# Attention and two MLPs on one core: both first token blocks cut in two for the first MLP, two scalars spread by TensorE, and new order lists

## The chip, the core and the metric

The kernel runs on one core of a Trainium2 chip. The core has TensorE (PE) for matrix products, VectorE (DVE) and ScalarE (ACT) for elementwise work, GpSimd (POOL), SyncE (SP), whose queue issues all of this kernel's transfers, and 16 DMA engines that carry them out. The metric is device time in microseconds (us); the time shown is the median of several runs.

## The reference

Three stages follow each other, in float32.

```python
# 1: attention in chunks of 32 with a window; q, k, v: (4, 8, 768, 64), mem_k, mem_v: 8 rows a head
for c in range(24):
    k_full = concat(mem_k, k[c*32 - 16 : c*32 + 40])      # 8 + at most 56 rows
    v_full = concat(mem_v, v[c*32 - 16 : c*32 + 40])
    a = softmax(q_c @ k_full.T / 8)                        # with 1e-9 added to the sum
    out[c] = a @ v_full
x = out as (3072, 512)
# 2: first MLP; w_in (512, 2048), w_out (2048, 512), s and b are single numbers
r = maximum(x @ w_in, 0)
y = (s * r * r + b) @ w_out
# 3: second MLP; w_gate, w_val (512, 1536), w_out2 (1536, 512)
g = y @ w_gate
result = (g * sigmoid(g) * (y @ w_val)) @ w_out2
```

## The kernel before, in words

The attention works on 24 groups of 128 tokens. A group has six stages, each named by a letter in the lists: Q (queries transposed), T (keys transposed and spread into one window per chunk), S (scores, maximum, shift, exp, sums), A (probabilities transposed), V (product with the values, normalised), X (the result transposed and rounded into a high part `xhi` and a low part `xlo`). Three groups make a token block t of 384 tokens; there are eight blocks. Groups 0 to 5 load whole rows (`load_tokens`, one transfer list K) and transpose on PE; later groups load k and q in 12 parts (`load_quadrant`) and transpose on DVE (`turn_queries`, `turn_keys`). Values are loaded by `load_values` (V in the list of loads) into two buffers, group g into buffer g % 2.

The first MLP goes through 16 hidden blocks m of 128 for each token block t. An up product U (`first_up`, 12 matmuls: each float32 product is made of three with split operands, lines 560 to 562) gives `hp`. Then come relu (`first_relu`), the square with s and b (`first_square`), rounding to `ghi` (`round_hi`) and the rest `glo` (`residue`), and a down product D (`first_down`, 12 matmuls) adds to four accumulators `acc0` to `acc3`. Four accumulators exist, so one token block at a time can collect its sum. When a run of hidden blocks of one token block ends, `first_out` copies the accumulators to `y` and `first_store` writes them to DRAM, as a part (`part_dram`) if hidden blocks are left, else as `y_dram`; a part is loaded again (`load_part0`) and added at the end. Before the change block 0 is cut behind hidden block 5 (`PART = 6`), so that the order is (0, 0 to 5), (1, 0 to 15), (0, 6 to 15), and then blocks 2 to 7 whole.

A weight block m (W in the list of loads, `load_w1`: 512 KB of `w_in` and 512 KB of `w_out`) is used first when its hidden block first comes up. Before that `split` turns it into a high and a low part: magnitude (ACT or DVE, lines 840 and 842), bound (846), shift (850), sign (855), rest (862), rounding to the high part (229 or 231, ACT or DVE), and the low part (904), all but the named choices on DVE. All 16 stay in SBUF; each token block uses all of them. The second MLP comes after the eighth block and has weights and lists of its own.

The instructions are first collected as tasks with lengths (`plan.add`), dependencies and buffer rings, and a list scheduler (`Plan.run`) then fixes the order on every engine; on the chip each engine runs its own list in that order and waits on semaphores. PE's order is the order in which tasks are added: for the start it is written out in `START` (U and D stand for the next up and down product), and later `VISITS` says at which half step which stage of a group comes. `LOADS` gives the order of the first transfers on SP, each issued behind the one before it. `MOVED` names the tasks that go to the other engine than usual, with ACT or DVE as the choice (`either`): `r`, `s`, `g` with t_m are relu, square and rounding, `h_first` and `m_first` rounding and magnitude of a weight block, `k`, `m`, `q`, `a`, `x` the copies of a group, `y` the copies out of the accumulators. The numbers s and b are broadcast over 128 partitions by two small transfers (`load_consts`), which have no place in `LOADS`.

## Time and profile before

| | |
|---|---|
| median of 3 runs | 1234.26 us (1233.92 to 1235.15) |
| the profiled execution, its own time | 1235.41 us |
| its span, from the first to the last instruction | 1233.6 us |
| mean granted TensorE clock | 0.989 |
| PE, DVE, ACT busy | 1189.7, 773.4, 506.3 us |

Busy times are those of the one profiled execution, and so are all start times, counted from the start of its span. Matmuls are pipelined, so the PE column tells when PE has work, not how well its array is used. PE idles or waits where its busy time in a window is less than the window.

### The profile page before, as it was taken

What the parts mean: (1) busy time and instruction counts of PE and PEld (TensorE: products, weight loads), DVE (VectorE), ACT (ScalarE), POOL (GpSimd) and SP (SyncE); (2) the same over time, 40 slices, a digit from 0 to 9 for tenths busy, and PEclk for the clock granted to TensorE, in tenths of its full rate; (3) what the DMA queues carried; (4) which work ended last, traced back from release to release, by engine and by line L of the source; (5) the groups of instructions that cost most, each with busy time, mean ns of one, the idle gap of its engine ahead of it and who ended that gap; (6) DMA issues with size and microseconds to landing.
All of it is one profiled execution on the core that took longest, in us unless ns stands there. A gap on an engine that the chain in (4) does not pass through costs nothing.

```text
span 1233.6 us, 25831 instructions
## 1 busy us (share of the span) xinstructions
PE 1189.7 (96%) x10296; PEld 1129.8 (92%) x10296; DVE 773.4 (63%) x1496; ACT 506.3 (41%) x1018; POOL 22.8 (2%) x54
## 2 busy tenths in 40 slices
...
GB/s 191 219 120 190 104 123 43 62 52 67 44 51 63 42 67 45 51 91 1 156 219 96 187 198 188 188 227 282 263 187 187 183 182 299 207 186 188 188 114 93
DMA packets 217128, 174.11 MB, mean 141 GB/s; under 512 B 157487, under 2 KB 188719, under 8 KB 215471
## 3 DMA queue, kind: packets, MB, share of 16 engines
...
q14 instruction: 41, 0.33, 0.1%
HBM read 124.40 MB, written 47.97 MB: 140 GB/s over the span
## 4 chain that ended last, share of the span: by engine, by line
PE 79%; SPq 9%; DMA 6%; DVE 3%; issue 2%; ACT 1%; DVEq 0%; ACTq 0%
PE chain_a L560 6%; PE chain_a L561 6%; PE chain_a L562 6%; PE oacc L561 5%; PE oacc L560 5%; PE oacc L562 5%; PE acc L560 5%; PE acc L561 5%; PE acc L562 5%; PE hp L560 5%; PE hp L562 5%; PE hp L561 5%; PE chain_b L561 4%; PE chain_b L562 4%; PE chain_b L560 4%; SPq L350 3%
## 5 line engine op out<-in xcount | busy, mean ns | idle before, releaser
L560 PE MATMUL acc<-ghi,w_first 128*128 128x384 f32 x512 | 176.0, 344 | 3.0 <-DVE ghi L231 1.8
L560 PE MATMUL hp<-xhi,w_first 128*128 128x384 f32 x512 | 175.7, 343 | 0.7 <-ACT xhi L229 0.7
L561 PE MATMUL acc<-glo,w_first 128*128 128x384 f32 x512 | 173.2, 338 | 2.5 <-DVE glo L622 1.1
L561 PE MATMUL hp<-xlo,w_first 128*128 128x384 f32 x512 | 172.6, 337 | 1.1 <-DVE xlo L553 1.1
L562 PE MATMUL hp<-xhi,w_first 128*128 128x384 f32 x512 | 172.5, 337 | 0.0
L562 PE MATMUL acc<-ghi,w_first 128*128 128x384 f32 x512 | 172.3, 337 | 0.0
L748 ACT ACTIVATE kept<-chain_a 128x256 f32<-128x256 f32 x216 | 83.0, 385 | 163.4 <-PE chain_a L562 134.4
L600 DVE SCALAR_TENSOR_TENSOR r<-r,s_sb 128x384 f32<-128x384 f32 x92 | 57.0, 620 | 107.8 <-ACT r L589 105.1
L589 ACT ACTIVATE r<-hp 128x384 f32<-128x384 f32 x96 | 47.1, 491 | 186.1 <-PE hp L562 179.1
L560 PE MATMUL oacc<-w_down,ghi 128*128 128x512 f32 x288 | 114.1, 396 | 0.1
L561 PE MATMUL oacc<-w_down,ghi 128*128 128x512 f32 x288 | 114.1, 396 | 0.0
L562 PE MATMUL oacc<-w_down,glo 128*128 128x512 f32 x288 | 112.0, 389 | 0.0
L560 PEld LDWEIGHTS acc<-ghi,w_first 128*128 128x128 f32 x512 | 96.8, 189 | 5.9 <-DVE ghi L231 2.8
L561 PEld LDWEIGHTS acc<-glo,w_first 128*128 128x128 f32 x512 | 97.0, 189 | 5.4 <-DVE glo L620 3.1
L560 PEld LDWEIGHTS hp<-xhi,w_first 128*128 128x128 f32 x512 | 97.3, 190 | 2.2 <-ACT xhi L229 0.9
L561 PEld LDWEIGHTS hp<-xlo,w_first 128*128 128x128 f32 x512 | 97.4, 190 | 1.3 <-DVE xlo L553 1.3
L562 PEld LDWEIGHTS hp<-xhi,w_first 128*128 128x128 f32 x512 | 97.1, 190 | 0.0
L562 PEld LDWEIGHTS acc<-ghi,w_first 128*128 128x128 f32 x512 | 96.8, 189 | 0.0
L765 DVE TENSOR_TENSOR v<-v,g 128x256 f32<-128x256 f32 x144 | 61.0, 424 | 52.3 <-ACT g L761 50.4
L753 DVE TENSOR_TENSOR v<-chain_b,kept 128x256 f32<-128x256 f32 x144 | 61.0, 423 | 41.5 <-PE chain_b L562 26.8
L773 DVE TENSOR_TENSOR glo<-v,ghi 128x256 fp32r<-128x256 f32 x144 | 60.6, 421 | 36.6 <-ACT ghi L229 36.6
L560 PE MATMUL chain_a<-y,hi_up 128*128 128x256 f32 x288 | 81.3, 282 | 0.6 <-ACT kept L748 0.5
...
## 6 DMA issues: line engine op xcount, KB each, us to landing
...
```

The lines of the kernel that those rows point to most:

```text
L350: nc.sync.dma_start(out=qin[:, j], in_=q[b, h, s0:s0 + GQ, ds].rearrange("(n t) i -> t n i", t=QUAD))
L560: nc.tensor.matmul(o, whi, xhi, start=first, stop=False, skip_group_check=onto)
L561: nc.tensor.matmul(o, whi, xlo, start=False, stop=False, skip_group_check=onto)
L562: nc.tensor.matmul(o, wlo, xhi, start=False, stop=last, skip_group_check=onto)
L589: nc.scalar.activation(out=r, in_=hp, func=AF.Relu)
L600: nc.vector.scalar_tensor_tensor(out=r, in0=r, scalar=s_sb[:, 0:1], in1=r, op0=ALU.mult, op1=ALU.mult)
L748: nc.scalar.activation(out=t, in_=st2[n]["A"], func=AF.Copy)
L753: nc.vector.tensor_tensor(out=t, in0=st2[n]["B"], in1=st2[n].pop(f"a{i}"), op=ALU.add)
L765: nc.vector.tensor_tensor(out=v, in0=v, in1=g, op=ALU.mult)
L773: nc.vector.tensor_tensor(out=lo, in0=st2[n].pop(f"v{half + 1}"), in1=st2[n][f"hi{half}"].bitcast(F32), op=ALU.subtract)
```

## The change

Both token blocks 0 and 1 are now cut in two, and the order of the hidden blocks is (0, 0 to 3), (1, 0 to 7), (0, 4 to 15), (1, 8 to 15), then blocks 2 to 7 whole as before. Block 1 gets a part in DRAM of its own, stored behind hidden block 7 and loaded and added at the end.

s and b are loaded as one number each into a tile of one partition, by two transfers that stand first in `LOADS` (C). Two matmuls with one row (`spread_consts`) spread them over 128 partitions into PSUM, and DVE copies them to SBUF. PE runs these two first.

For a group that `MOVED` names with e (group 1), the shift by the maximum, the exp and the sums are done by eight ACT instructions, one for each head, with the negative maximum as bias and the sum as second output; DVE makes the negative maximum, and keeps only the last two small operations of the sums.

`START`, `VISITS`, `LOADS` and `MOVED` are new. Of MOVED, with names for the first two blocks and six groups, these go: a1, g0_5, g0_6, g0_10, g0_11, g0_15, g1_0, g1_2, g1_5, g1_9, g1_10, g1_11, h_first1, h_first6, h_first9, h_first12, h_first14, k2_0, k3_0, k4_0, m1_0, m2_0, m4_1, m_first0, q2, q4, r0_0, r0_12, r0_13, r1_5, s0_11, s0_12, s0_13, s1_2, s1_3, x4, y1_15_1, y1_15_2. These come: e1, g0_7, g0_14, g1_4, g1_12, g1_13, h_first10, k0_0, k1_1, k3_1, k5_0, k5_1, m2_1, m3_0, m5_0, m_first4, m_first7, m_first14, q3, r0_14, r1_3, r1_11, r1_14, s0_3, s0_4, s0_5, s0_6, s0_14, s1_0, s1_8, s1_9, s1_13, s1_15, x0, y0_3_0, y0_3_1, y0_3_3, y1_7_0. The usual engine of s0_4 and s0_5 changes from ACT to DVE.

```diff
@@ -28,35 +28,36 @@
 
 
 START = (
-    "Q0 T0 S0 Q1 A0 V0 T1 S1 X0 Q2 T2 A1 S2 V1 X1 A2 V2 Q3 T3 X2 S3 U U Q4 D T4 U A3 S4 D V3 "
-    "U D A4 Q5 T5 X3 U V4 X4 D U S5 D A5 D V5 X5 U "
+    "Q0 T0 S0 Q1 T1 A0 V0 S1 Q2 T2 S2 A1 X0 V1 A2 X1 V2 Q3 X2 U U D T3 D S3 Q4 U A3 V3 T4 U "
+    "X3 S4 D Q5 A4 V4 T5 S5 X4 D A5 V5 X5 U "
 )
 
 VISITS = {
-    (True, 0): (-3, -4, -3, 1, 8, 15),
-    (True, 1): (2, 6, 9, 15, 17, 18),
-    (True, 2): (10, 16, 17, 22, 25, 31),
+    (True, 0): (-10, -6, -3, 1, 6, 15),
+    (True, 1): (-1, 10, 9, 15, 21, 23),
+    (True, 2): (11, 9, 21, 26, 29, 31),
     (False, 0): (-8, -2, -3, 2, 8, 11),
     (False, 1): (6, 6, 8, 12, 18, 21),
     (False, 2): (10, 18, 18, 25, 29, 30),
 }
 
 LOADS = (
-    "W0 K0 W1 V0 K1 K2 W2 V1 W4 V2 K3 W3 V3 K4 W6 K5 W5 V4 W8 V5 W7 W10 W9 "
+    "C K0 V1 K1 W0 V0 K2 V2 W3 W1 K3 W2 V4 K4 W5 V3 K5 W4 V5 W6 W7 W8 W10 W9 "
 )
 
 MOVED = (
-    "a1 a11 a12 a2 a6 g0_10 g0_11 g0_13 g0_15 g0_2 g0_3 g0_4 g0_5 g0_6 g1_0 g1_10 g1_11 g1_15 "
-    "g1_2 g1_3 g1_5 g1_8 g1_9 g2_1 g2_10 g2_12 g2_15 g2_2 g2_3 g2_6 g2_7 g2_8 g3_0 g3_1 g7_1 "
...
+    "a11 a12 a2 a9 e1 g0_13 g0_14 g0_2 g0_3 g0_4 g0_7 g1_12 g1_13 g1_15 g1_3 g1_4 g1_8 g2_0 "
+    "g2_1 g2_10 g2_12 g2_15 g2_2 g2_3 g2_6 g2_7 g2_8 g3_0 g3_1 g7_1 g7_11 g7_15 g7_3 g7_7 "
...
 )
 
 
@@ -189,7 +190,8 @@
     GPB = T // GQ
     NG = NB * GPB
     NSUB = T // P
-    PART = 6
+    SEGMENTS = ((0, 0, 4), (1, 0, 8), (0, 4, M1), (1, 8, M1), *((t, 0, M1) for t in range(2, NB)))
+    SPLIT = {t: [a for n, a, z in SEGMENTS if n == t and a] for t in range(NB)}
     CH = 2 * 512
     TS = 512
     TH = TS // 2
@@ -212,10 +214,11 @@
 
     ident = const.tile([P, P], F32, name="ident")
     make_identity(nc, ident)
-    s_sb = const.tile([P, 1], F32, name="s_sb")
-    b_sb = const.tile([P, 1], F32, name="b_sb")
+    sb_in = const.tile([1, 2], F32, name="sb_in")
+    sb = const.tile([P, 2], F32, name="sb")
+    s_sb, b_sb = sb[:, 0:1], sb[:, 1:2]
     y_dram = [dram.tile([P, KD, T], F32, name=f"y_dram{t}") for t in range(NB)]
-    part_dram = dram.tile([P, KD, T], F32, name="part_dram")
+    part_dram = {t: dram.tile([P, KD, T], F32, name=f"part_dram{t}") for t in range(NB) if SPLIT[t]}
     sum_dram = [
         [dram.tile([P, TS // P, DM], F32, name=f"sum_dram{h}_{s}") for s in range(NS)] for h in range(PASSES - 1)
     ]
@@ -253,8 +256,17 @@
         raw1[m] = load_slot((w_in[:, cols], w_out[cols, :]), f"first{m}")
 
     def load_consts():
-        for dst, src in ((s_sb, s_in), (b_sb, b_in)):
-            nc.sync.dma_start(out=dst, in_=src.unsqueeze(0).to_broadcast([P, 1]))
+        for n, src in enumerate((s_in, b_in)):
+            nc.sync.dma_start(out=sb_in[:, n:n + 1], in_=src.unsqueeze(0))
+
+    spread = []
+
+    def spread_consts():
+        spread.append(ps_h.tile([P, 512], F32, tag="h", name="spread")[:, 0:2])
+        for n in range(2):
+            nc.tensor.matmul(
+                spread[0][:, n:n + 1], sb_in[:, n:n + 1].to_broadcast([1, P]), ident[0:1, 0:1], start=True, stop=True
+            )
 
     def weight1(m, n):
         w = w1[m]
@@ -487,6 +499,19 @@
         sc = staged[g]["sc"].rearrange("p j e s -> p (j e s)")
         nc.scalar.activation(out=sc, in_=sc, func=AF.Exp, scale=SCALE)
 
+    def stage_below(g):
+        staged[g]["nb"] = nb = ap_.tile([P, 2, NP, 1], F32, tag="nb", name=f"nb{g}")
+        nc.vector.tensor_scalar(nb, staged[g].pop("mx"), -SCALE, None, op0=ALU.mult)
+
+    def stage_exp_heads(g, e):
+        if e == 0:
+            staged[g]["rc"] = ap_.tile([P, NP, 2, 1], F32, tag="rc", name=f"rc{g}", bufs=2)
+        for j in range(NP):
+            nc.scalar.activation(
+                out=scores_to(g)[:, j, e], in_=staged[g]["s"][e][:, j], func=AF.Exp, scale=SCALE,
+                bias=staged[g]["nb"][:, e, j], accum_out=staged[g]["rc"][:, j, e],
+            )
+
     def stage_probs(g, early):
         sc = staged[g]["sc"]
         ps = bank(ps_acc, "acc3", f"psA{g}") if early else bank(ps_a, "a", f"psA{g}")
@@ -516,12 +541,14 @@
         stage_values(g, both)
         stage_scores(g + 1, both)
 
-    def stage_sums(g):
-        staged[g]["rc"] = rc = ap_.tile([P, NP, 2, 1], F32, tag="rc", name=f"rc{g}", bufs=2)
-        flat = rc.rearrange("p j e o -> p (j e o)")
-        nc.vector.tensor_reduce(
-            out=flat, in_=staged[g]["sc"].rearrange("p j e s -> p (j e) s"), op=ALU.add, axis=AX.X
-        )
+    def stage_sums(g, done=False):
+        if not done:
+            staged[g]["rc"] = ap_.tile([P, NP, 2, 1], F32, tag="rc", name=f"rc{g}", bufs=2)
+        flat = staged[g]["rc"].rearrange("p j e o -> p (j e o)")
+        if not done:
+            nc.vector.tensor_reduce(
+                out=flat, in_=staged[g]["sc"].rearrange("p j e s -> p (j e) s"), op=ALU.add, axis=AX.X
+            )
         nc.vector.tensor_scalar(flat, flat, 1e-9, None, op0=ALU.add)
         nc.vector.reciprocal(flat, flat)
 
@@ -567,10 +594,10 @@
 
 
     def begins(t, m):
-        return m == 0 or (t == 0 and m == PART)
+        return m == 0 or m in SPLIT[t]
 
     def ends(t, m):
-        return m == M1 - 1 or (t == 0 and m == PART - 1)
+        return m == M1 - 1 or m + 1 in SPLIT[t]
 
     def first_up(t, m):
         whi, wlo = weight1(m, 0)
@@ -595,12 +622,12 @@
         r, _ = g_t[t, m]
         if engine == "ACT":
             nc.scalar.activation(out=r, in_=r, func=AF.Square)
-            nc.scalar.activation(out=r, in_=r, func=AF.Identity, scale=s_sb[:, 0:1], bias=b_sb[:, 0:1])
+            nc.scalar.activation(out=r, in_=r, func=AF.Identity, scale=s_sb, bias=b_sb)
         else:
             nc.vector.scalar_tensor_tensor(
-                out=r, in0=r, scalar=s_sb[:, 0:1], in1=r, op0=ALU.mult, op1=ALU.mult
-            )
-            g_t[t, m] = r, b_sb[:, 0:1]
+                out=r, in0=r, scalar=s_sb, in1=r, op0=ALU.mult, op1=ALU.mult
+            )
+            g_t[t, m] = r, b_sb
 
     def round_hi(engine, t, m):
         r, bias = g_t[t, m]
@@ -635,18 +662,18 @@
 
     def first_out(engine, t, m, i):
         y = gp.tile([P, T], F32, tag="r", name="y")
-        if t == 0 and m == M1 - 1:
+        if t in parts:
             nc.vector.tensor_tensor(out=y, in0=acc[t, i], in1=parts[t][:, i], op=ALU.add)
         else:
             copy(engine, y, acc[t, i])
         y_t[t, i] = y
 
     def first_store(t, m, i):
-        nc.sync.dma_start(out=(y_dram[t] if m == M1 - 1 else part_dram)[:, i, :], in_=y_t.pop((t, i)))
-
-    def load_part0():
-        parts[0] = wp.tile([P, KD, T], F32, tag="w", name="part")
-        nc.sync.dma_start(out=parts[0], in_=part_dram)
+        nc.sync.dma_start(out=(y_dram[t] if m == M1 - 1 else part_dram[t])[:, i, :], in_=y_t.pop((t, i)))
+
+    def load_part(t):
+        parts[t] = wp.tile([P, KD, T], F32, tag="w", name="part")
+        nc.sync.dma_start(out=parts[t], in_=part_dram[t])
 
     y_t = {}
     sp = None
@@ -981,6 +1008,13 @@
             t = plan.add(PE, 1.00, lambda: stage_scores(g), at_[g]["t"], take=["a", "a"], give=["kt", "qt"])
         t = plan.add(DVE, 0.34, lambda: stage_max(g, 0), [t])
         t = plan.add(DVE, 0.34, lambda: stage_max(g, 1), [t])
+        if f"e{g}" in moved:
+            t = plan.add(DVE, 0.07, lambda: stage_below(g), [t])
+            for e in range(2):
+                t = plan.add(ACT, 1.0, lambda e=e: stage_exp_heads(g, e), [t], give=give, take=own if e == 0 else ())
+            at_[g]["n"] = t
+            at_[g]["rc"] = plan.add(DVE, 0.22, lambda: stage_sums(g, True), [t])
+            return t
         for e in range(2):
             t = plan.add(DVE, 0.34, lambda e=e: stage_shift(g, e), [t], give=give, take=own if e == 0 else ())
         at_[g]["n"] = plan.add(ACT, 0.54, lambda: stage_exp(g), [t])
@@ -1036,8 +1070,8 @@
     split1 = {}
     g_ready = {}
     acc_free = []
-    part_stored = []
-    part_loaded = []
+    part_stored = {}
+    part_loaded = {}
     y_stored = {}
 
     def plan_w1(m):
@@ -1055,16 +1089,18 @@
         )
         e = either(f"r{t}_{m}", {ACT: 0.52, DVE: 0.47}, lambda e: first_relu(e, t, m), [u], take=["r"], give=["h"])
         e = either(
-            f"s{t}_{m}", {ACT: 1.30, DVE: 0.56} if t == NB - 1 or (t == 0 and m < PART) else
+            f"s{t}_{m}", {ACT: 1.30, DVE: 0.56} if t == NB - 1 or (t == 0 and m < SEGMENTS[0][2]) else
             {DVE: 0.56, ACT: 1.30}, lambda e: first_square(e, t, m), [e, consts],
         )
         e = either(f"g{t}_{m}", {ACT: 0.55, DVE: 0.47}, lambda e: round_hi(e, t, m), [e], take=["ghi"])
         g_ready[t, m] = plan.add(DVE, 0.52, lambda: residue(DVE, t, m), [e], take=["glo"], give=["r"])
 
     def plan_down1(t, m):
-        added = t == 0 and m == M1 - 1
+        added = m == M1 - 1 and SPLIT[t]
         if added:
-            part_loaded.append(transfer([*part_stored, split1[M1 - 1]], load_part0, 1, 768, ["w"]))
+            part_loaded[t] = transfer(
+                [*part_stored[t], split1[M1 - 1]], lambda: load_part(t), 1, 768, ["w"], name=f"part{t}"
+            )
         outs = []
         for i in range(KD):
             last = i == KD - 1
@@ -1081,14 +1117,14 @@
             e = either(
                 f"y{t}_{m}_{i}", {DVE: 0.5} if added else {DVE: 0.5, ACT: 0.43} if i % 2 else
                 {ACT: 0.43, DVE: 0.5}, lambda e, i=i: first_out(e, t, m, i),
-                [outs[i], *(part_loaded if added else ())], take=["r"],
+                [outs[i], *([part_loaded[t]] if added else ())], take=["r"],
             )
             acc_free.append(e)
             stored = transfer([e], lambda i=i: first_store(t, m, i), 1, 192, give=["r"])
             if m == M1 - 1:
                 y_stored[t, i] = stored
             else:
-                part_stored.append(stored)
+                part_stored.setdefault(t, []).append(stored)
         if added:
             plan.add(DVE, 0.01, None, acc_free, put=["w"])
 
@@ -1225,11 +1261,10 @@
             plan.add(DVE, 0.01, None, partial[h, s], put=["w"], give=["so"])
 
 
-    consts = transfer([], load_consts, 2, 1)
-    order = (
-        [(0, m) for m in range(PART)] + [(1, m) for m in range(M1)] + [(0, m) for m in range(PART, M1)]
-        + [(t, m) for t in range(2, NB) for m in range(M1)]
-    )
+    consts = transfer([], load_consts, 2, 1, name="C")
+    consts = plan.add(PE, 0.10, spread_consts, [consts], take=["h"])
+    consts = plan.add(DVE, 0.10, lambda: nc.vector.tensor_copy(sb, spread[0]), [consts], give=["h"])
+    order = [(t, m) for t, a, z in SEGMENTS for m in range(a, z)]
     ups = downs = 0
     for item in START.split():
         what, g = item[0], int(item[1:] or 0)
```

## Rows read from the trace of the kernel before

**Rows 1.** The page: busy time of the engines, share of the span, instructions.
```profile
PE 1189.7 (96%) x10296; PEld 1129.8 (92%) x10296; DVE 773.4 (63%) x1496; ACT 506.3 (41%) x1018; POOL 22.8 (2%) x54
```

**Rows 2.** Windows: us, busy PE, PEld, DVE, ACT, POOL (instructions), granted clock, DMA share, GB/s.
```profile
0.00:20.00 20.00, 5.00 (x83) 4.36 (x84) 12.47 (x23) 4.64 (x5) 2.85 (x12) 1.00 0.88 207
20.00:40.00 20.00, 12.03 (x288) 9.72 (x287) 14.41 (x32) 5.87 (x10) 2.16 (x6) 0.92 0.77 179
...
60.00:80.00 20.00, 17.71 (x286) 15.74 (x284) 19.62 (x35) 12.26 (x21) 0.00 (x0) 1.00 0.57 140
80.00:100.00 20.00, 15.32 (x193) 13.79 (x194) 18.88 (x34) 8.13 (x12) 0.00 (x0) 0.87 0.47 119
...
sum 160.00, PE 124.72 PEld 113.49 DVE 135.43 ACT 69.98 POOL 13.46; mean PE 15.59 PEld 14.19 DVE 16.93 ACT 8.75 POOL 1.68
...
97.00:168.00 71.00, 68.16 (x544) 64.09 (x545) 64.74 (x95) 32.90 (x49) 8.46 (x12) 0.98 0.53 147
sum 168.00, PE 132.56 PEld 120.41 DVE 143.36 ACT 72.01 POOL 13.46; mean PE 44.19 PEld 40.14 DVE 47.79 ACT 24.00 POOL 4.49
...
169.00:546.00 377.00, 374.58 (x3961) 367.06 (x3960) 196.63 (x400) 125.46 (x226) 9.29 (x24) 1.00 0.28 58
```

**Rows 3.** Waits of PE, 160 to 640 us: in total, times, longest.
```profile
PE acc L560 <- DVE ghi L231: 1.6, 1, 1.6
```

**Rows 4.** Timeline of PE: start, us, instruction, [idle before <- releaser].
```profile
8.34 1.09 PE L415 MATMUL psQ<-ident,qk 128*128 128x128 f32 x4 [8.34 <-DMA qk<-in_q_dram]
...
36.12 1.48 PE L511 MATMUL psV<-v,at 64*32 64x64 f32 x37 [2.43 <-DMA v<-in_v_dram]
...
50.59 0.69 PE L560 MATMUL hp<-xhi,w_first 128*128 128x384 f32 x1
...
97.15 0.44 PE L560 MATMUL hp<-xhi,w_first 128*128 128x384 f32 x1 [0.69 <-ACT xhi L229]
...
168.00 0.33 PE L560 MATMUL hp<-xhi,w_first 128*128 128x384 f32 x1
...
176.32 0.33 PE L560 MATMUL hp<-xhi,w_first 128*128 128x384 f32 x1
```

**Rows 5.** Timeline of SP's queue: start, us, issue.
```profile
3.02 0.44 SPq L285 DMA_DIRECT2D qk<-in_q_dram  x1
...
27.79 0.40 SPq L257 DMA_DIRECT2D s_sb<-in_moe_s_dram  x1
...
29.81 7.36 SPq L401 DMA_DIRECT2D v<-in_v_dram  x8
...
153.43 0.39 SPq L240 DMA_DIRECT2D raw_first<-in_moe_w_in_dram  x1
...
170.29 1.50 SPq L649 DMA_DIRECT2D part<-part_dram  x1
```

**Rows 6.** Groups by line and shape, 0 to 97 us: busy us, mean ns.
```profile
L855 DVE SCALAR_TENSOR_TENSOR raw_first<-raw_first,t_first 128x1024 uint32<-128x1024 uint32 x9 | 11.0, 1220 | 0.2
...
L850 DVE TENSOR_SCALAR t_first<-t_first 128x1024 uint32<-128x1024 uint32 x9 | 6.2, 690 | 0.2
...
L229 ACT ACTIVATE kt<-psK 128x64 f32<-128x64 f32 x6 | 1.4, 225 | 2.5 <-DVE kt L231 2.5
...
L598 ACT ACTIVATE r<-r,b_sb,s_sb 128x384 f32<-128x384 f32 x5 | 3.5, 709 | 0.2
```

**Rows 7.** Timeline of DVE.
```profile
159.95 0.69 DVE L846 TENSOR_SCALAR t_first<-t_first 128x1024 f32<-128x1024 f32 x1 [2.24 <-ACT t_first L840]
...
166.54 1.22 DVE L904 TENSOR_TENSOR w_first<-raw_first,w_first 128x1024 fp32r<-128x1024 f32 x1
```

**Rows 8.** Windows of 2.5 us, columns as in rows 2.
```profile
32.50:35.00 2.50, 1.19 (x65) 0.89 (x64) 2.40 (x7) 0.23 (x1) 0.00 (x0) 1.00 1.11 361
35.00:37.50 2.50, 1.32 (x37) 1.07 (x37) 2.46 (x7) 1.11 (x2) 0.00 (x0) 0.85 1.00 140
```

**Rows 9.** Window behind the waits of step 6.
```profile
97.00:102.00 5.00, 3.76 (x12) 3.51 (x13) 4.50 (x5) 1.27 (x3) 0.00 (x0) 0.66 0.95 282
```

19 rows, old and new, of the table MOVED are left out of this document.

## The prediction

> **What bounds the kernel now.** I read the page first: TensorE (PE) is busy for 96% of the span, so only its gaps can be won [rows 1]. The windows show where they are: up to 160 us PE works 124.7 us, so 35.3 us are idle, 15 of these in the first 20 us, 8 in the second, 2.3 in 60 to 80 and 4.7 in 80 to 100; from 169 to 546 us it idles 2.4 us of 377 [rows 2], with one wait of 1.6 us as the longest [rows 3]. So the argument is about the first 180 us. I call one up product with its down product a step; (t, m) is token block t with hidden block m, W0 to W15 are the weight blocks, and steps are numbered from 0 in the order in which they run.
>
> PE's own rows, in order of time, show what the start is made of [rows 4]. The first transpose waits until 8.34 us for group 0's q, the values of group 1 land for 36.12, and the first up product starts at 50.59. Step 6, which is (1,0) and needs all of block 1's x, starts at 97.15 behind a wait on ACT for that x. Step 21, the first use of W15, starts at 168.00, and step 23 at 176.32: 8.32 for two steps, so 2.08 us a product at full clock. Two engines stand behind these. SP needs 7.36 us to issue V2's eight loads, of 0.4 each when nothing is in the way [rows 5]. And VectorE (DVE) is busy 19.6 of 20 us in 60 to 80 [rows 2]: each weight block costs it five passes over 128x1024, two like L850 (0.69) and three like L855 (1.22) [rows 6]; the last pass of the last block begins at 166.54 and takes 1.22 [rows 7]. PE asks for that block at 168.00, so DVE is just in time there and sets the pace.
>
> **The change, part by part.**
>
> *Loads.* Ahead of V2 the old list has W0, W1, W2 and W4 (4.2 MB), the new one W0 alone. Ahead of V5 the old one has eight weight blocks, the new one six. The bytes taken out are the quick ones: with the 16 DMA engines full, weights landed at 361 GB/s in one window, where values landed at 140 in the next [rows 8]. So 3.1 MB less in front of V2 buy 3.1/0.34 = 9 us. By the mean of 207 and 179 GB/s of the first two windows [rows 2] it would be 16; but K3 (below), behind two weight blocks, would then land at 42, and the first up product would start at 45. The Trainium skill says why the two differ ("DMA: Bandwidth & Descriptors", Specifications and Why small descriptors are slow: pieces under 512 B miss line rate, and a head's row here has 256 B); the trace agrees, with 140 against 361.
>
> SP in the new order, at 0.44 an issue [rows 5]: C two issues, K six, W two, V ten or eight with stalls. C to 1.6, K0 to 4.3, V1 to 9, K1 to 11.5, W0 to 12.5, V0 to 18.5, K2 to 21. V2 reuses V0's buffer and waits for V0's product, about 22.3, so it goes to 26; W3 and W1 to 28, K3 to 30.6. Behind 2.1 MB of weights at 0.34 MB/us and its own 0.6 MB, K3 lands near 37.5.
>
> *The start.* PE's order ends "V2 Q3 X2 U". V0 lands near 20.5, and for the chain of products and copies from there to group 2's values I allow 16 us; the old run came to group 1's values at 36.12 because they landed only then [rows 4]. So Q3 runs at 37.5, X2 at 38.4, and behind it and the two x copies, 2.1 us together by estimate, the first up product starts at 40.5 instead of 50.59: 10.1 us earlier. T3 and S3, done before it in the old order, come behind it now: 1.6 us by estimate, two stages of some 0.8. Net 8.5. Bounds: 37 (K3 no obstacle, gain 12) and 46 (V loads stall as V2 did, gain 3).
>
> *x of block 1.* It is needed at step 4 instead of 6. From 50.59 to 97.15 PE had 12 products of 2.08 and 15 stages of attention to do, at some 0.8 each 12 us: 37 of 46.6 us: 9.6 us were lost to DVE. The new stretch has 8 products, the 12 and the 1.6: 30.3 us, so by PE alone step 4 could start at 70.8. DVE's prices: a weight block 4.7 (its five passes, 5.04, times 0.93, since neighbours overlap by some 0.08 each). Up to 97 us it did 143.4 - 64.7 = 78.6 us of work [rows 2]; 43 passes (four kinds nine times, one seven [rows 6]) and two roundings take 42, five steps 6, so a group of attention 30.6/6 = 5.1. From 97 to 168, 38 passes and five roundings take 39, 1.6 groups 8, and the other 18 over 15 steps are 1.2 a step. From 40.5 it then has to do a rest of W1 (2), W2 and W3 (9.4), three groups (15.5), four steps (4.8) and a copy: 32.2 us, 34 to 36 at the 91 to 96% at which it ran. Step 4 starts at 75.5. Less the two steps that come later (8.35), the old 97.15 corresponds to 88.8: gain 13.3 there.
>
> *W15.* It is wanted at step 23 instead of 21. DVE did 143.4 us of work up to 168 [rows 2]. The new order adds two steps (2.4). The new lists, counted by name for the first two blocks, take from DVE 4 roundings of weights and 2 q or at copies (0.68 each), 6 roundings of g (0.35), a net squaring with scale (0.62) and for group 1 two shifts and a sum (1.4), and give it 2 magnitudes (0.69) and 2 k copies (0.62): 5.6 times 0.93 less. That makes 140.6. DVE's idle time was 24.6: 13.1 in the first 40 us and 11.5 behind them [rows 2]. In the new order the first 40 us hold fewer weights to fill them with (15 idle), and behind I take 5 to 13. W15 is ready between 161 and 169; I take 166, nearer the old share. Gain 176.3 - 166 = 10. This is less than the 13.3 at step 4, so it counts: PE gives some 3 us back in steps 16 to 23, where each step wants 4.7 plus 1.2 us of DVE and takes PE some 4.4.
>
> *s and b.* Two issues move from 27.8 [rows 5] to the head: 0.8 us of SP ahead of K0, contained in the sum. The two one-row products and the copy of two columns stand in no row. Below, nothing: PE idles until group 0 lands at 8.34 [rows 4]. Above, a copy of 0.22 [rows 6] for each of the three, 0.7, if a late landing of C takes that cover away. I take nothing.
>
> *Group 1's exp by heads.* Eight ACT instructions of 128x64. The nearest row, a copy of that size, takes 0.22; one with two pointer operands takes 0.71 at 128x384 [rows 6]: 1.8 to 3 us ahead of A1, in place of two shifts and one exp, some 1.4. K3 lands only at 37.5, so I take nothing; without that cover it would be 0.4 to 1.6.
>
> *Second split.* Block 1 is cut too: four more stores, a load of 1.5 on SP [rows 5], four adds in place of copies, one more change of accumulators. At the old changes PE has another up product in between, which hides it. I take nothing. The load of block 0's part is now close: it waits for the slot that W15's split frees, and its sum is wanted some 8 us behind that. Bounds 0 and 3 us, the latter if group loads stand before it on SP.
>
> *Later blocks.* Same work, and the lists hardly differ. The group loads on SP start perhaps 4 us earlier while PE is 10 earlier. The stall of 1.6 [rows 3] may go, others may come: plus or minus 2.
>
> **Sum.** The profiled run took 1235.4 us for a span of 1233.6, 1.2 over the median of 1234.3. 1235.4 - 10 = 1225.4, against the median 1224.3. I say 1225.
>
> **The rivals.**
>
> *DVE loses it to late loads.* It waited 2.24 us for W15's load [rows 7] and 6.3 in all from 97 to 168 [rows 2]. If that comes to 9 or 10, and PE's waits are each followed by a slow stretch as from 97 to 102 (granted 0.66, so part of it at 1.2 of the 2.4 GHz [rows 9], some 1.7 us lost), W15 is ready at 169 to 171 and the gain is 3 to 6: 1229 to 1232. For it: ten blocks instead of eight now come behind V5, on a queue that also carries the group loads. Against: two steps more of slack. The Trainium skill names the slow stretches ("TensorE: Matmul & The Clock Gate", Part 1: idleness halves the clock, work restores it); the trace agrees, at 0.66 behind the waits of step 6.
>
> *Slower: W15 issued too late.* It was issued at 153.43 and ready at 167.76: 14.3 us [rows 5, 7]. If the new plan issues it after 162, behind ten weights, a part's load and the group loads on the same queue, it is ready after 176.3 and the whole gain is gone; each us more is a us lost. Issued at 165 to 172, it gives 1237 to 1244. Against: SP reaches the group loads earlier, with V5.
>
> *More: DVE is not the limit.* If it idles only 10 us before 40, W15 is ready by 160, and step 4's gain of 13, or 16 with a start at 38, counts: 1218 to 1221.
>
> **How the numbers follow.** Forecast, 1221 to 1229: 0.48. More: 0.14. Gain lost, 1229 to 1234: 0.20. Slower: 0.18. A measurement of this kernel tells about 0.2% from no change, 2.5 us, so faster means under 1231.8: 0.48, 0.14 and just over half of the third, 0.73. Within: 0.10. Slower: 0.17. Likeliest 1225, by itself 1221 to 1229. For 8 in 10 I leave out a little of "more" and the far half of "slower": 1217 to 1238.
>
> **What would show it.** Right: group 0's first transpose at 6.5 to 8; first up product near 40; step 4 near 75; DVE over 93% busy from 60 to 160; W15's last pass ending near 166 with step 23 right behind it; PE idle up to 160 us near 25 in place of 35. Wrong: a first up product past 46, with PE waiting on v or qk loads; DVE idle before a weight's first pass; PE waits on block 0's part or on r buffers at a change of accumulators; new waits past 200 us behind the turning of keys.

## Result and profile after

The changed kernel took 1241.12 us (median of 5 runs, 1239.87 to 1243.8) beside 1234.26 of the kernel before (5 runs, 1232.25 to 1235.56): ratio 1.006, 95% interval 1.0045 to 1.0075. It is 7 us slower, where 1225 was forecast and 1238 was the end of the range. The profiled execution took 1243.8 for a span of 1242.0, 8.4 us over that of before.

The windows of after, columns as in [rows 2]:

```profile
0.00:20.00 20.00, 8.34 (x102) 6.81 (x102) 7.65 (x19) 4.40 (x7) 5.55 (x18) 1.00 0.71 156
20.00:40.00 20.00, 12.37 (x345) 9.53 (x342) 13.72 (x30) 6.85 (x23) 0.40 (x1) 0.92 0.79 198
...
60.00:80.00 20.00, 15.04 (x266) 13.58 (x256) 17.94 (x34) 7.14 (x15) 0.00 (x0) 0.83 0.64 166
80.00:100.00 20.00, 15.03 (x184) 13.49 (x184) 18.77 (x33) 8.81 (x14) 0.00 (x0) 0.74 0.45 131
...
sum 160.00, PE 125.37 PEld 114.36 DVE 132.94 ACT 75.05 POOL 14.59; mean PE 15.67 PEld 14.30 DVE 16.62 ACT 9.38 POOL 1.82
...
169.00:546.00 377.00, 370.21 (x3809) 361.61 (x3808) 193.88 (x391) 127.61 (x232) 10.38 (x24) 1.00 0.28 59
```

PE gained 3.3 us of busy time in the first 20 us and lost it between 60 and 100, where it is also slower: busy time times granted clock is 15.04 x 0.83 + 15.03 x 0.74 = 23.6 us there, against 17.71 + 15.32 x 0.87 = 31.0 in [rows 2]. And from 169 to 546 us it idles 6.8 us instead of 2.4.

PE's timeline, the places of [rows 4]: group 0's and group 3's queries, step 0, step 4 (the first of block 1, which was step 6), step 23.

```profile
5.99 1.11 PE L427 MATMUL psQ<-ident,qk 128*128 128x128 f32 x4 [2.96 <-DMA qk<-in_q_dram]
...
41.67 1.11 PE L427 MATMUL psQ<-ident,qk 128*128 128x128 f32 x4 [3.11 <-DMA qk<-in_q_dram]
44.33 0.69 PE L587 MATMUL hp<-xhi,w_first 128*128 128x384 f32 x1 [0.69 <-ACT xhi L232]
...
93.39 0.44 PE L587 MATMUL hp<-xhi,w_first 128*128 128x384 f32 x1 [0.69 <-ACT xhi L232]
...
178.73 0.33 PE L587 MATMUL hp<-xhi,w_first 128*128 128x384 f32 x1
```

SP issued W15 and block 0's part, and DVE ran the last pass of W15, at these times ([rows 5, 7]):

```profile
160.02 0.39 SPq L243 DMA_DIRECT2D raw_first<-in_moe_w_in_dram  x1
...
178.44 0.35 SPq L676 DMA_DIRECT2D part<-part_dram  x1
```
```profile
177.23 1.18 DVE L931 TENSOR_TENSOR w_first<-raw_first,w_first 128x1024 fp32r<-128x1024 f32 x1
```

PE's waits from 160 to 640 us, in place of the one of [rows 3]:

```profile
PE acc L587 <- ACT ghi L232: 2.8, 1, 2.8
PE acc L587 <- ACT ghi L638: 2.2, 2, 1.8
PE acc L588 <- DVE glo L649: 0.8, 4, 0.2
PE acc L587 <- DVE ghi L640: 0.6, 1, 0.6
```

So the loss has two parts. Step 0 is 6.3 us earlier than before, step 6 5.8 later, step 23 2.4 later; from there the lag grows to 8.3 at step 83 and stays. The second MLP adds nothing.

### The profile page after: what moved, and what is told of

Read it like the earlier page. It is cut to its first block, busy times and chain, and to the rows that moved or that the text cites. A ratio compares the mean times of both kernels' runs of the same rounds, so it can differ in the third digit from the quotient of the medians.

```text
span 1242.0 us, 25859 instructions
## 1 busy us (share of the span) xinstructions
PE 1194.4 (96%) x10300; PEld 1133.6 (91%) x10300; DVE 768.8 (62%) x1489; ACT 516.2 (42%) x1045; POOL 25.0 (2%) x54
## 3 DMA queue, kind: packets, MB, share of 16 engines
q1 hardware_dynamic: 217442, 174.02, 44.7%
## 4 chain that ended last, share of the span: by engine, by line
PE 81%; SPq 9%; DMA 5%; DVE 3%; issue 2%; ACT 1%; DVEq 0%; ACTq 0%
PE chain_a L587 6%; PE chain_a L588 6%; PE acc L588 6%; PE chain_a L589 6%; PE hp L587 5%; PE acc L587 5%; PE acc L589 5%; PE oacc L588 5%; PE hp L589 5%; PE oacc L587 5%; PE hp L588 5%; PE oacc L589 5%; PE chain_b L588 4%; PE chain_b L589 4%; PE chain_b L587 4%; SPq L362 3%
## 5 line engine op out<-in xcount | busy, mean ns | idle before, releaser
L627 DVE SCALAR_TENSOR_TENSOR r<-r,sb 128x384 f32<-128x384 f32 x90 | 55.6, 617 | 107.8 <-ACT r L616 107.2
```

Source lines behind the costliest of these rows:

```text
L627: nc.vector.scalar_tensor_tensor(out=r, in0=r, scalar=s_sb, in1=r, op0=ALU.mult, op1=ALU.mult)
```

## Experiments

All but the named part is the changed kernel ("after") or the kernel before; the numbers are those of the names (there are no 9 and 10). Each kernel ran 4 to 12 times, with before beside it. The table gives the ratio with its interval and, from the one profiled execution of each, how much earlier (-) or later a step starts than in before, in us, worked out from the timelines of PE. The first row is before itself. Pairs with the same order up to 110 us (after and 11; before and 12) differ by up to 1.8 us at step 0, so less than 2 us at one step is not read. Executions of one kernel lie 2.3 (7) to 9.6 us (19) apart, and the profile of 17 is the fastest of its six; times are therefore compared by the ratios.

```
kernel              ratio [95%]             step 0      4      6     16     23     31     48     83
before                                       50.59  75.30  97.15 143.94 176.32 215.09 298.00 460.75
after               1.0060 [1.0045,1.0075]   -6.26  18.09   5.82   3.22   2.41   2.12   4.86   8.28
1  part_pool        1.0044 [1.0028,1.0060]   -5.07  16.85   4.40   1.65   0.84   1.45   2.75   5.50
2  x_first          1.0158 [1.0141,1.0174]   -7.53  12.46   0.33   1.48  10.95  13.13   9.20  16.91
3  both of these    1.0155 [1.0138,1.0171]   -6.64  12.20  -0.54   0.81  11.73  13.38   9.58  21.19
4  sb_only          1.0044 [1.0031,1.0056]   -2.01  -2.14  -3.11  -2.50   0.54   0.55   2.36   5.16
5  loads_only       1.0085 [1.0066,1.0103]   -0.63   1.54   4.93   3.94  14.20  14.38  12.44  12.92
6  cut_only         1.0110 [1.0092,1.0128]   -5.75  21.01   9.32  11.13  10.31  10.03   8.10  11.91
7  v_pool           1.0040 [1.0028,1.0053]   -6.19  14.59   2.89   0.87   3.33   4.06   1.30   2.42
8  before, v_pool   1.0041 [1.0027,1.0056]   -1.99  -1.88  -2.73  -4.76   6.47   6.47   2.55   1.44
11 v_pool_free      1.0019 [1.0007,1.0031]   -4.67  18.06   5.83   3.14   2.40   2.18   0.96   1.69
12 before, the same 1.0008 [0.9992,1.0023]   -1.75  -0.81  -1.29   0.27  -0.17  -0.16   0.09   0.90
13 less_dve         1.0024 [1.0011,1.0036]   -5.00  15.36   1.73  -1.89  -2.70  -2.95   0.61   2.24
14 11 without e1    1.0018 [1.0005,1.0032]   -6.36  16.03   3.91   3.78   3.02   2.76   3.30   4.62
15 cover_six        1.0055 [1.0039,1.0071]   -5.59   0.38   4.80   8.11   8.92   8.66   8.45   8.61
16 old_lists_6_8    1.0042 [1.0026,1.0059]   -1.87  -1.49   2.65   0.94   2.25   2.85   2.02   3.02
17 old_lists_6_10   1.0055 [1.0035,1.0075]   -2.11  -1.68  -3.18  -4.28  -1.19   1.58   2.22   3.05
18 old_cut_v_pool   0.9982 [0.9970,0.9995]   -1.55  -1.10  -2.33  -2.76  -2.13  -2.12  -1.81  -1.52
19 t3_s3_first      1.0000 [0.9986,1.0014]   -4.19  14.48   2.81   0.46  -0.34  -0.03  -2.12  -0.08
```

### 1 to 3: the part's load, and x ahead of the weights

In after SP stood from 171.1 to 178.44 at the load of block 0's part, and DVE split W4, W5 and most of W6 ahead of block 1's x.

```diff
-        nc.sync.dma_start(out=parts[t], in_=part_dram[t])
+        nc.gpsimd.dma_start(out=parts[t], in_=part_dram[t])
...
```
```diff
...
+    plan.chain += [(x_parts[1][-1], firsts[f"first{m}"]) for m in range(4, M1)]
```

Part's load on GpSimd: 

> The changed kernel, but the two part loads are issued by GpSimd instead of SP. Theory 1 (SP stands 7.3 us at the load of block 0's part, waiting for the slot of W15, and all group loads behind it are late from then on, so that DVE later stalls at the turning of queries): SP has no gap over 2 us from 165 to 185 us, group 9's queries are turned near 197 instead of 203.5, the four DVE waits of 2.3, 4.7, 3.5 and 4.9 us before a turning fall to 6 us or less in all, and the time falls by 3 to 6 us, to 1235 to 1238. Rival (the turnings stall because the plan puts them too early whatever SP does): the waits stay over 12 us in all, and the time within 1 us of the changed kernel's 1241. Steps 0 to 23 stay as they are under both.

W4 to W15 split only behind block 1's x: 

> The changed kernel, but planned so that DVE and ACT begin no split of W4 to W15 before the x of block 1 is complete. Theory 2 (step 4 comes at 93.4 instead of 75 because DVE splits W4, W5 and most of W6, some 13 us, ahead of block 1's x): step 4 starts at 80 to 85, step 6 at 90 to 95 instead of 103, and the time falls by 5 to 10 us, to 1231 to 1236, if the later weights still come in time. Rival A (8 products are too little cover, and the chain of 15 attention stages sets step 4 by its own waits): step 4 stays at 90 or later, and with the splits pushed back the weights are late: PE waits in steps 8 to 23, 1241 to 1250. Rival B (the loads of V3 and V5 set it): step 4 at 84 to 88.

Both: 

> Both edits at once: part loads issued by GpSimd, and no split of W4 to W15 before block 1's x is complete. If theories 1 and 2 hold and add up: 1227 to 1232, under the kernel before. If only theory 1 holds: 1236 to 1245. If a gain at the start makes the group loads on SP relatively later and is lost again at the turnings: within 2 us of the run with the part loads alone, with DVE waits before turnings of 10 us or more in all.

The first moved group 9's turning (of its queries, on DVE) only from 203.5 to 202.1 us, and the lag still grows by 4.1 us from step 31 to 83, where it grew by 6.2 in after: SP's stand is at most a small part of it. In the second, step 4 came 5.6 us earlier (87.76) although DVE now waits in that stretch, as its timeline shows:

```profile
68.58 0.62 DVE L627 SCALAR_TENSOR_TENSOR r<-r,sb 128x384 f32<-128x384 f32 x1 [3.23 <-ACT r L616]
...
85.16 0.76 DVE L558 TENSOR_TENSOR on<-psV,rc 128x256 f32<-128x256 f32 x2 [2.06 <-PE psV L536]
```

So DVE's splits are a part of the delay and not its floor, and pushed back they make the later weights late: step 23 at +10.95. The third is no faster than the second: the two cures do not add up.

### 4 to 6: the change in parts

Old cut, old tables and old lists with s and b as one pair at the head of the loads (4); that with the new list of loads (5, the pair ahead of K0 as in after); the new cut and tables with the old loads (6, without the heads' exp, old engine list but for two copies of block 1's accumulators).

```diff
-    SEGMENTS = ((0, 0, 4), (1, 0, 8), (0, 4, M1), (1, 8, M1), *((t, 0, M1) for t in range(2, NB)))
+    SEGMENTS = ((0, 0, 6), (1, 0, M1), (0, 6, M1), *((t, 0, M1) for t in range(2, NB)))
...
```

> The kernel before in cut, START, VISITS and MOVED, with s and b loaded as one number each at the head of the loads, spread by PE and copied by DVE. All theories: the same as before within 1.5 us (1233 to 1236), since the three small instructions fit into the wait for group 0 and SP is held 0.6 us. Rival: moving 0.6 us of SP to the head shifts every later load, and the planner's order with it, by enough for other waits: off by 3 us or more either way.

> The kernel after with the old cut (6 products of block 0, all of block 1, the other 10 of block 0) and the old stage tables; of the lists the list of loads alone is new. Theory 1 (the new list of loads is what hurts: quadrant loads of group 6 ahead of V2, V4, V3, V5 on SP's queue): slower than before by 4 to 8 us, 1238 to 1242, with most of the loss by the step that was at 165 us. Rival (the loss of the kernel after lies in the cut: block 1's x has only 8 products as cover): this kernel is within 3 us of before, 1231 to 1237, since W15 now lands early and the wait of 2.3 us for it near 167 us, which the kernel with the old lists of everything shows, is gone.

> The kernel after with its new cut and stage tables, but with the old list of loads (the pair of s and b at its head) and the old engine list. Theory 1 (the list of loads hurts): step 4, the first product of block 1, starts at 85 us or before instead of 93.4, and the time is 1232 to 1237. Rival (the cut itself: block 1's attention chain and DVE set step 4): step 4 within 3 us of 93.4, late weights cost more, 1240 to 1248.

The loads alone and the cut alone each lose more than both together, so their losses do not add up, and neither is the cause by itself. Kernel 5 loses most of it at W15, which SP's timeline has issued only at 165.72: +3.7 us at step 20, +14.2 at step 23. In 6, step 4 comes 2.9 us later still than in after, as its rival had it. Kernel 4 was the surprise: without cut and without new loads it is slower too. Its timeline of PE shows two things. What it gains by step 16 goes at W15:

```profile
166.99 0.44 PE L586 MATMUL hp<-xhi,w_first 128*128 128x384 f32 x1 [1.15 <-DVE w_first L233]
168.78 0.44 PE L588 MATMUL hp<-xhi,w_first 128*128 128x384 f32 x1 [1.18 <-DVE w_first L930]
280.27 0.69 PE L586 MATMUL acc<-ghi,w_first 128*128 128x384 f32 x1 [2.23 <-ACT ghi L231]
430.88 0.44 PE L586 MATMUL acc<-ghi,w_first 128*128 128x384 f32 x1 [2.51 <-ACT ghi L637]
```

And the two last lines are the later loss of after, at the same groups (12 and 18), in a kernel without the cut.

### 7, 8, 11, 12: value loads off SP's queue

From 180 us on a group's loads take SP about as long as PE takes for the group. In after, SP's timeline from the values of group 11 to those of group 12 (some 35 lines between, most of 0.3 to 0.5 us an issue, and none starts more than 0.1 us behind the end of the one before it), then DVE, ACT and PE behind it:

```profile
252.90 4.22 SPq L413 DMA_DIRECT2D v<-in_v_dram  x10
257.21 0.27 SPq L348 DMA_DIRECT2D kin<-in_mem_k_dram  x1
...
277.94 0.43 SPq L362 DMA_DIRECT2D qin<-in_q_dram  x1
278.47 0.28 SPq L402 DMA_DIRECT2D v<-in_mem_v_dram  x1
```
```profile
279.66 0.71 DVE L368 STREAM_TRANSPOSE qt<-qin 128x512 f32<-128x512 f32 x1 [4.66 <-DMA v<-in_v_dram]
```
```profile
281.13 0.95 ACT L232 ACTIVATE kt<-kT 128x896 f32<-128x896 f32 x1 [7.11 <-DVE kT L374]
...
283.27 0.52 ACT L232 ACTIVATE ghi<-r 128x384 fp32r<-128x384 f32 x1
```
```profile
283.84 0.44 PE L587 MATMUL acc<-ghi,w_first 128*128 128x384 f32 x1 [2.84 <-ACT ghi L232]
```

This round of 54 issues takes SP 25.6 us; PE took (460.75 - 298.00) / 35 = 4.65 us a step in the kernel before, 24.8 for the 16/3 steps of a group. A round has 44 to 56 issues, and the stalls of DVE and PE lie at the longest (groups 11, 12, 17 and 18); the twelve rounds from 226.0 to 523.0 us take 24.75 on the mean, so SP has nothing to spare. DVE's wait is put down to the values; the queries, whose last issue is at 277.94, are what the instruction reads. ACT has the spread keys ahead of a ghi, and PE stands 2.84 us.

```diff
+        issuer = nc.gpsimd if g >= EARLY else nc.sync
-                        nc.sync.dma_start(
+                        issuer.dma_start(
...
-                    vv = transfer([], lambda: load_values(g), 8, 460, take=["v"], rate=180.0, name=f"V{g}")
+                    issue = issues[f"V{g}"] = plan.add("POOL", 4.0, lambda: load_values(g), [], ["fly"], take=["v"])
+                    vv = plan.add(MOVE, 460 / 180.0, None, [issue], put=["fly"], lag=1.8)
```

> The kernel after with the value loads of groups 6 and later issued by GpSimd instead of SP. Theory 1 (from 180 us on SP's issues are the pace: one group's quadrant and value loads take it about as long as PE takes for the group's share of products, so a late group 7 never heals): DVE's waits ahead of the turning of queries, 15.4 us in sum in the kernel after, fall under 5 us, the steps lose no more than 3 us between 180 us and step 83 instead of 6, time 1235 to 1238. Rival (the later loss is set by the order of DVE's list and by PE's own waits, not by SP): waits and time stay, 1240 to 1242.

> The kernel before with the value loads of groups 6 and later issued by GpSimd. Theory 1 (SP's pace): DVE's waits ahead of the turning of queries, 7.7 us in sum in the kernel before, fall under 3 us; PE stands only 2.6 us between 160 and 640 us in the kernel before, so the gain is 0.5 to 2.5 us, 1232 to 1234. Rival (GpSimd's issues are slower and the values land late): PE waits on the values' products and the time is 1236 or more.

In 7 DVE's waits ahead of the turning of queries fell to 0.4 us and nothing was lost between steps 31 and 83, but five waits of 0.9 us of score products for the spread keys came in their place (PE's waits, 160 to 640 us):

```profile
PE psB L470 <- ACT kt L232: 3.6, 4, 0.9
PE acc L588 <- DVE ghi L641: 1.4, 1, 1.4
PE psB L470 <- DVE kt L234: 1.0, 1, 1.0
```

Both times lie in the rivals' ranges, though the shorter waits of theory 1 were there. Kernel 8 was 5.1 us ahead at step 20 and lost 11.5 at W15: W14's last pass ended at 156.6, W15 was issued at 157.10, and PE stood.

```profile
171.72 0.69 PE L561 MATMUL hp<-xhi,w_first 128*128 128x384 f32 x1 [9.15 <-DVE w_first L231]
```

The next two count the value loads in the planner without one of the two places for transfers in flight, and with 5.0 us for the issues of a group instead of 4.0; nothing else differs from 7 and 8.

```diff
-                    issue = issues[f"V{g}"] = plan.add("POOL", 4.0, lambda: load_values(g), [], ["fly"], take=["v"])
-                    vv = plan.add(MOVE, 460 / 180.0, None, [issue], put=["fly"], lag=1.8)
+                    issue = issues[f"V{g}"] = plan.add("POOL", 5.0, lambda: load_values(g), [], take=["v"])
+                    vv = plan.add("MOVEV", 460 / 180.0, None, [issue], lag=1.8)
```

> The kernel after with the value loads of groups 6 and later issued by GpSimd, as in the run before it, but counted in the planner without one of the two places for transfers in flight, so that DVE's and ACT's order of the first 170 us stays that of the kernel after. Theory 1 (SP's issues are the pace from 180 us on, and the five waits of 0.9 us of score products for the spread keys in the last run came from the planner's order): step 23 starts 1 to 3 us later than before, nothing more is lost between there and step 83 (1 us at most), time 1235 to 1237.5. Rival (GpSimd's issues bring waits of their own): new waits of score or value products, 1239 to 1242.

> The kernel before with the same. Theory 1: DVE's waits ahead of the turning of queries (7.7 us) go, PE stands under 1 us between 160 and 640 us instead of 2.6, and the start is that of the kernel before: 1232.5 to 1235. Rival: as for the run above, waits of score or value products for keys or values, 1236 to 1240.

In 11 the lag at step 83 is 1.7 us instead of 8.3, with that at step 23 unchanged at 2.4: the later loss is gone, and it was SP's pace (the ratio falls with it, from 1.0060 to 1.0019). DVE's waits ahead of turnings did not vanish (3.72 at group 12), but the turnings come 3.6 us earlier, early enough for PE. SP's and DVE's timelines of 11:

```profile
253.61 0.28 SPq L348 DMA_DIRECT2D kin<-in_mem_k_dram  x1
...
274.07 0.43 SPq L362 DMA_DIRECT2D qin<-in_q_dram  x1
```
```profile
276.06 0.71 DVE L368 STREAM_TRANSPOSE qt<-qin 128x512 f32<-128x512 f32 x1 [3.72 <-DMA qin<-in_q_dram]
```

The median of 11 was 1238.44, 1 us over what theory 1 gave. In 12, where before had only 2.6 us of PE's waits to lose, no change can be told. The Trainium skill ("DMA: Bandwidth & Descriptors", Issuing engines are not separate DMA queues) says that issuing from several engines saves the sequencer's time alone, which is usually small beside the transfer. The trace agrees that it is this time that was saved: the DMA engines were 28% busy from 169 to 546 us. One issue is short beside its transfer here as well (some 0.6 us of 2.5 from issue to landing, for a value load from GpSimd in 11); what counted is that SP has 44 to 56 of them to do one behind the other for each group.

### 13 and 14: DVE's share, and the exp by heads

```diff
-        t = plan.add(DVE, 0.60, bound, [t])
-        t = plan.add(DVE, 0.72, shift, [t])
+        late = name.startswith("first") and int(name[5:]) >= 4
+        t = plan.add(DVE, 0.60, None if late else bound, [t])
+        t = plan.add(DVE, 0.72, None if late else shift, [t])
```

> The kernel after without two of DVE's seven passes (the bounding and the shift, 0.69 us each) in the splits of W4 to W15; the engines' order is kept. The low bits of these weights are then not those of the reference. It is a measurement of DVE's share: 12 times 1.4 us, 17 us less on DVE before step 23. Theory 2 (DVE's total sets both step 4 and step 23): step 4 starts at 86 to 89 us instead of 93.4, step 23 at 168 to 172 instead of 178.7, time 1229 to 1235. Rival (the chain of loads and of PE's own attention stages sets them): step 4 within 2 us of 93.4, W15 not issued before 157, time 1239 to 1243.

> The first of these runs with group 1's exponential in one instruction again, as in the kernel before, instead of 8 by heads with 8 read-outs of sums. Theory 1 (the exponential by heads costs the start: S2 waited 2.5 us for the queries' copy that ACT held behind it): step 0 starts 1.5 to 3 us earlier than 44.3 and the time is 1 to 3 us under that of the first run. Rival (it takes 1.3 us of DVE's work off and gives as much as it costs): within 1 us of the first run.

Kernel 13 leaves out two passes over each of these weights and so computes with other weights; only its times are used. With 17 us less on DVE up to step 23, step 4 came 2.7 us earlier and step 23 5.1 us; the time, 1238.55, fell between the two expectations. The 5.1 us are there by step 16 (-1.89 against 3.22) and do not grow up to step 23, which PE reached at 173.62 without a wait. So in after, too, step 23 was late by what came ahead of step 16, not by W15. With the value loads still on SP, 13 loses 4.9 us between steps 23 and 83 again. The heads' exp made no difference, as the rival had it: 1.0018 against 1.0019.

### 15 to 19: cover, second split, order of the stages

Two more products as cover, in 15; the second split with the old lists, at 8 and at 10, and the old cut as their control (16 to 18); group 3's keys and scores ahead of the first product again (19). All with the value loads as in 11; 16 to 18 also have two entries less in the old engine list (copies of block 1's accumulators, y1_15_1 and y1_15_2), which in 18 are then made by the other engine than in before, 4 and 12. In 17 the table of stages for groups 6 and 7 differs too.

```diff
-    "X3 S4 D Q5 A4 V4 T5 S5 X4 D A5 V5 X5 U "
+    "X3 S4 D Q5 A4 U V4 T5 S5 X4 D A5 U D V5 X5 D U "
...
```
```diff
+    SEGMENTS = ((0, 0, 6), (1, 0, 10), (0, 6, M1), (1, 10, M1), *((t, 0, M1) for t in range(2, NB)))
...
-    (True, 0): (-3, -4, -3, 1, 8, 15),
-    (True, 1): (2, 6, 9, 15, 17, 18),
+    (True, 0): (-3, -4, -3, 1, 8, 19),
+    (True, 1): (2, 6, 9, 15, 21, 23),
```
```diff
-    "Q0 T0 S0 Q1 T1 A0 V0 S1 Q2 T2 S2 A1 X0 V1 A2 X1 V2 Q3 X2 U U D T3 D S3 Q4 U A3 V3 T4 U "
+    "Q0 T0 S0 Q1 T1 A0 V0 S1 Q2 T2 S2 A1 X0 V1 A2 X1 V2 Q3 T3 X2 S3 U U D Q4 D U A3 V3 T4 U "
```

> The kernel after with value loads of groups 6 and later on GpSimd, with the first cut at 6 instead of 4: products 4 and 5 of block 0 stand between the attention stages of groups 4 and 5. Theory (cover): the granted clock between 60 and 90 us is 0.9 or more, step 6 (block 1's first) starts at 94 to 98 us as in the kernel before (97.15) with two more steps done than in the kernel after, step 20 comes 1 to 4 us earlier than before, and the time is 1231 to 1236 unless W15 is waited for. Rival (the two products delay the attention stages as much as they cover, since DVE has W4 and W5 to split first): step 6 at 101 us or later, time 1237 to 1242.

> The old lists and stage tables with s and b as one pair, first cut at 6, and block 1 split at 8; value loads of groups 6 and later on GpSimd. Theory (the second split takes W15's wait away and costs nothing itself): the 2 to 3 us that the old lists with the pair gain by step 16 are still there at step 31 and at the end, 1231 to 1235. Rival (the part's copies, stores and its load cost what the wait did): steps fall behind between 14 and 24 by 3 us or more, 1236 to 1242.

> The run before with block 1 split at 10 instead of 8, so that W15 is met at step 25 (187 us) instead of 23 (176), and groups 6 and 7 put into x later by the table. Theory: as the run before, and no wait for W15 at all, 1230 to 1234. Rival (late x of block 2 or late parts): a wait at step 26 to 32, 1236 to 1242.

> The control: old cut and old lists with s and b as one pair and the value loads of groups 6 and later on GpSimd. Both theories: the start 2 to 3 us earlier by step 16, given back at W15's first product (step 21 or 22) where PE waits 2 to 4 us, no later loss, 1233 to 1236.

> The kernel after with value loads of groups 6 and later on GpSimd (the run whose steps 31 to 83 lose nothing), with the keys and scores of group 3 put ahead of the first up product in PE's order again, as in the kernel before. Theory (the stages of groups 3 to 5 are a chain of hand-overs that runs at its own pace, so whatever stands ahead of them delays block 1's x): step 0 starts 1.5 to 4 us later than the 45.9 of that run, step 4 starts 3 to 6 us earlier than its 93.4, at 87 to 90, and the time is 1233 to 1236. Rival (only DVE's and the loads' work by then counts, in whatever order PE runs): step 4 within 1.5 us of 93.4, step 0 later, time 1238 to 1240.

15 went the rival's way: step 6 at 101.95, and a wait of 5.8 us for a ghi behind it, although the granted clock from 60 to 90 us is 0.94, as the theory wanted. 16 and 17 are slower than their control. 16 is 5.0 us behind 18 at step 6 already, long before its second split at step 14: PE waits there for the values of group 5 (3 us between 91 and 94 us) and for x. It therefore does not tell what the split costs. 17 runs like 18 or ahead of it up to step 16 and loses 5.9 us by step 31, where 18 loses 0.6. Some of 17's waits of PE are these, at the down product of step 17, the second behind the change of accumulators, and at W15, which is met at step 25:

```profile
151.77 0.44 PE L587 MATMUL acc<-ghi,w_first 128*128 128x384 f32 x1 [1.11 <-ACT ghi L231]
153.25 0.44 PE L588 MATMUL acc<-glo,w_first 128*128 128x384 f32 x1 [1.03 <-DVE glo L647]
...
185.80 0.44 PE L587 MATMUL hp<-xhi,w_first 128*128 128x384 f32 x1 [0.75 <-DVE w_first L233]
187.59 0.44 PE L589 MATMUL hp<-xhi,w_first 128*128 128x384 f32 x1 [1.18 <-DVE w_first L931]
```

18 is the only version faster than the kernel before: 1233.33 us, ratio 0.9982, interval 0.997 to 0.9995, a small gain for the best of 17 kernels. It has neither cut nor new lists of loads: only the pair s and b, the value loads off SP, and the two copies on the other engine. The wait of 2 to 4 us for W15 that was expected did not come: between steps 20 and 23 it loses 0.6 us, where 4 loses 2.3. The later loss of 4, 4.6 us from step 31 to 83, is 0.6 in 18, as 11 had shown for after. 19 keeps the change and is as fast as before (ratio 1.0000): step 4 at 89.78, 3.6 us earlier than in 11, with step 0 only 0.5 us later. So the value loads off SP and T3 and S3 in their old place take back the whole loss (1.0060, 1.0019, 1.0000), and the gain that was forecast does not come with them.

```profile
45.01 1.47 PE L470 MATMUL psS<-kt,qt 64*32 64x64 f32 x64 [1.59 <-DVE kt L234]
...
89.78 0.69 PE L588 MATMUL hp<-xhi,w_first 128*128 128x384 f32 x1 [0.69 <-ACT xhi L232]
```

## Why the prediction was wrong

*Loads and the start: right in kind, short in size.* The first transpose at 5.99 lies just under the 6.5 to 8 given, the first up product at 44.33 within 37 to 46: 6.3 us gained, where 10.1 were taken (8.5 net). Group 3's q landed for 41.67, not 37.5. SP's timeline tells why: quadrant loads of group 6, which stood in no sum, came between K2 and V2, and V2 was issued up to 29.7 us, not 26.

```profile
21.36 0.47 SPq L348 DMA_DIRECT2D kin<-in_mem_k_dram  x1
...
25.35 4.39 SPq L413 DMA_DIRECT2D v<-in_v_dram  x8
```

*"x of block 1" is the step that failed first.* Step 4 was to start at 75.5, by a sum of DVE's work alone, and started at 93.39, 17.9 us later: in place of a gain of 13.3 us the lag at step 6 is 5.8. Of the 17.9 us, 3.8 are the later first product. The other 14.1 lie in the stretch from step 0 to block 1's first product, which the sum had at 35 us and which took 49.1. The windows of that stretch in after, in 2 (W4 to W15 split behind x), in 15 (12 products in it) and in before (12 as well; us, busy PE, PEld, DVE, ACT, POOL, granted clock, DMA share, GB/s):

```profile
44.33:93.39 49.06, 37.63 (x536) 33.63 (x536) 43.73 (x76) 24.25 (x39) 0.00 (x0) 0.80 0.64 156
43.06:87.76 44.70, 35.28 (x537) 31.14 (x537) 31.16 (x62) 19.85 (x35) 0.00 (x0) 0.90 0.68 168
45.00:101.95 56.95, 43.60 (x584) 38.83 (x585) 52.77 (x89) 27.38 (x42) 11.60 (x19) 0.94 0.71 177
50.59:97.15 46.56, 39.93 (x514) 36.19 (x512) 42.55 (x76) 24.82 (x41) 0.00 (x0) 0.93 0.60 142
```

The sum had two errors. The first is DVE's work: it left out that DVE would split W4, W5 and most of W6 ahead of x, 27 passes over weights where the sum has about 12, so that DVE was busy 43.7 us and not 32.2. Run 2 takes these passes out. Its DVE does what the sum said (31.2 us, 12 passes), and the stretch is 4.4 us shorter (4.0 in 13, with shorter splits). The second error is larger: with the very work of the sum, run 2 still needs 44.7 us for the 35. The sum took the stages of groups 3 to 5 as work that packs, by PE at 30 us and by DVE at 35; they hand over between PE, DVE and ACT, and each of these waits for the others. PE's work was counted rightly for full clock (37.63 us at a granted clock of 0.80 are 30.1), but at 0.80 it took 7.3 us more, and PE idled 11.4 us. PE's timeline of after shows such waits between 59 and 94 us:

```profile
59.26 0.84 PE L469 MATMUL psS<-kt,qt 64*32 64x64 f32 x62 [2.00 <-ACT kt L232]
...
80.30 0.83 PE L438 MATMUL psK<-ident,qk 80*128 80x80 f32 x8 [1.66 <-DVE on L558]
82.52 0.39 PE L469 MATMUL psS<-kt,qt 64*32 64x64 f32 x2 [1.39 <-DVE kt L234]
...
92.05 0.66 PE L567 MATMUL psO<-ident,on 128*128 128x128 f32 x4 [1.02 <-DVE on L558]
```

The kernel before needs 46.6 us with 12 products and idles 6.6 of them, at 0.93. That the missing cover is the cause is not shown, though: with 12 products again, 15 has its clock back (0.94), but idles 13.4 us, and its DVE is busy 52.8 us of 56.9. One piece is shown: T3 and S3, counted at 1.6 us of PE, cost 3.6 us at step 4 (19 against 11). What else in the new order of stages, loads and engines makes PE wait stays open; no run takes the chain itself apart. Of the prediction's signs, DVE's share of over 93% from 60 to 160 us came true (94.5%), and PE's idle time up to 160 us stayed at 34.6 us where 25 were forecast: a busy DVE does not show that the rest packs behind it.

*W15: a size that did not come to count.* It was ready at 178.4, not 166, issued at 160.02, close to the condition of the rival "W15 issued too late" (after 162, ready after 176.3), and the measured time lies in that rival's range (1237 to 1244). But its mechanism is not what happened: in run 13 PE arrives 5.1 us earlier and finds W15 ready, and in after PE comes to it just as it is ready, late by what lies ahead of step 16. That the time came out in that range is chance. Where W15 is met at step 21, PE does wait for it: 2.3 us in 4 and 9.4 in 8, whose starts are quicker, and in 5, where it is issued at 165.72 and the rival's mechanism is there.

*"Later blocks, plus or minus 2" failed as well*, with 5.9 us between steps 23 and 83. The prediction weighed when SP's loads would start, and not SP's time for one group (24.75 us on the mean, 25.6 in the round shown) against PE's (24.8); waits behind the turning of keys were among its signs of being wrong. With no slack, a start whose turnings come 2 to 9 us later (group 8's at 176.61 instead of 169.53) is never made up, and the stalls at groups 12 and 17 to 18 reach PE. Run 11 takes them away. Kernel 4 shows that this needs no cut; which of the earlier shifts sets it off in each list was not settled.

*The rest.* The exp by heads cost nothing (14), as said. "Second split: nothing" stays open: with the old lists 17 lost 5.9 us between steps 16 and 31 and 18 only 0.6, with waits behind the change of accumulators and at W15, but the planner reorders all engines with it, and its table for groups 6 and 7 differs. "s and b: nothing" was, if anything, too low for the start: 4, which has nothing else, is 2.5 us ahead of before at step 16, and 18 is 3.0 us ahead of 12 (0.9982 against 1.0008 in the end), though the order of the engines changed with it.
